# First batch token-major, its value loads moved to the Pool queue ahead of the first weights, second weights in two halves, dummy matmuls at the start

## Chip, cores, metric

One core of a Trainium2 chip. The time is the device time of one execution in microseconds (us), lower is better. Every run of a kernel is correct against the reference unless said otherwise. A ratio is the mean time of one kernel's runs over that of the other's of the same rounds, so it is not quite the ratio of the medians quoted beside it.

## The reference

Forgetting attention, then a gated feed-forward block on its output:

```python
# q, k, v: (8 batches, 8 heads, 576 tokens, 64), f: (8, 8, 576)
scores = scale * q @ k.T
cum    = cumsum(log(clip(f, 1e-4, 1.0)))
scores = where(causal, -1e9, scores + cum_i - cum_j)
attn   = exp(scores - max); attn = attn / (sum + 1e-9)
x      = (attn @ v) reshaped to (4608 tokens, 512)
gate   = sigmoid(x @ w_gate)          # 512 x 1536
out    = (gate * (x @ w_val)) @ w_out # 1536 x 512
```

## The kernel before

It is scheduled by hand: the order of the program text is the order on each engine's queue. Scores are computed transposed (keys on partitions), ACT takes the exp, Pool (GpSimd) masks the diagonal blocks, PE multiplies with values that DVE or Pool scaled by the decay. The attention of the first batch runs alone (the opening); then each later batch is woven into the feed-forward chunks of 512 tokens, step by step. Loads with a cast from float32 to bf16 are issued by Pool, in line with its masks.

```python
def load_w1(c0, c1):                 # two issues on Pool
    cs = slice(c0, c1)
    for src, part in ((moe_w_gate, LO), (moe_w_val, HI)):
        nc.gpsimd.dma_start(w1[part, :, cs], src.rearrange("(s p) c -> p s c", p=64)[:, :, cs])

def load_w2(gi):                     # one issue on Pool: output weights "wo"
    nc.gpsimd.dma_start(wo[:, 4 * gi:4 * gi + 4, :], ...)

def S_unit(p, u, slot, tag=None):    # one unit of scores of head pair p
    ...                              # matmuls into ps
    nc.scalar.activation(e[...], ps[...], ACTF.Exp, scale=scale)
    nc.gpsimd.affine_select(out=m, in_=m, ...)      # the mask, on Pool

# the opening
nc.sync.dma_start(f_nat, ...)
load_v(0, 0, 4, range(NJT), nc.sync)        # values of heads 0-3 on SP
load_qk(0, 0, ((0, 2), (2, 4)))             # Pool
make_identity(nc, ident_bf)
load_qk(0, 1, ((0, 4),))
make_identity(nc, ident_f)
load_v(0, 4, 8, range(NJT), nc.gpsimd)      # values of heads 4-7 on Pool
load_w1(0, 512)
... (four pairs: units U, V, W; sums and values with tokens on columns) ...
load_w1(1024, 1536)

# the weave of the first chunk; put(step, what)
put(12, rest_values)                        # PE needs the masked eD, eA, eB of the rest units
for x, w in enumerate((5, 9, 12)):
    put(w, lambda x=x: load_w2(x))          # on Pool, between masks
```

A 64-token rest of each pair (unit Z, tiles eD, eA, eB, eC) is computed in the weave.

The softmax here doesn't subtract the row's maximum and nothing guards it: scores larger than these inputs give would overflow.

## Time and profile before

| | before |
|---|---|
| time | 374.13 us median of 3 (373.37 to 374.95) |
| span of the profiled execution | 373.4 us, granted clock 0.998 |
| PE busy | 359.3 us (96%) |
| opening ends (transposes of the second batch begin on PE) | 28.6 us |
| first sigmoid on ACT | 28.50 us |

The prediction below shows the stages, the chain of waits and the timeline of the opening. Two more views of this kernel are needed later. First, the page's line of the chain that ended last, by engine, which says that almost nothing but PE sets the end:

```profile
PE 94%; ACT 2%; DMA 1%; issue 1%; DVE 1%; POOL 0%; ACTq 0%; POOLq 0%
```

Second, the timeline of Pool at the first output weights (columns: start us, length us, engine, line, operation, out<-in, shapes, count, and in brackets the idle time before it and what ended it):

```profile
33.97 0.76 POOL L155 DMA_DIRECT2D wo<-in_moe_w_out_dram  x1 [2.09 <-DMA w<-in_moe_w_val_dram]
...
37.92 0.29 POOL L248 TENSOR_SCALAR_AFFINE_SELECT eB<-eB 64x128 bf16<-64x128 bf16 x1 [0.39 <-ACT eB L246]
```

Pool stands still 2.09 us before it can issue the load of wo, until a load of w issued earlier (at 24.91) has landed. The masks stand behind it in the same queue. Here it costs nothing: the last eB mask is waiting for ACT, not for Pool, and PE begins `rest_values` at 37.90 in one burst.

### The profile page before, as it was taken

How to read it: one execution, taken by the hardware profiler on the slowest of the kernel's cores; microseconds unless marked ns; L12 is line 12 of the kernel's file. 1: busy time of each engine (PE TensorE's matmuls, PEld its weight loads, DVE VectorE, ACT ScalarE, POOL GpSimd, SP SyncE). 2: the span in 40 equal slices, each digit the busy share in tenths (PEclk: the TensorE clock that was granted, in tenths of full speed). 3: DMA queues.
4: the chain of work that ended last, by engine and by line, in shares of the span. 5: the costliest groups of instructions: out<-in, count | busy, mean ns of one | idle time of the engine just before them, and what ended most of it. 6: DMA issues, size and time to landing. Idle time of an engine off the chain costs nothing.

```text
span 373.4 us, 12210 instructions
## 1 busy us (share of the span) xinstructions
PE 359.3 (96%) x5259; PEld 192.0 (51%) x5264; DVE 176.5 (47%) x382; ACT 195.7 (52%) x294; POOL 168.3 (45%) x265
## 2 busy tenths in 40 slices
PE   2889999999999999999999999999999999999996
PEld 1547545455555545454665566545456544444442
DVE  5775482557375555274708370737064703312320
ACT  5868754574736472848374727471747313323321
POOL 8896745064826663559665946460415000000000
PEclk9999999999999999999999999999999999999999
DMA  8999999599988976789984996596313131011002
GB/s 157 233 209 256 194 182 217 173 213 154 158 164 196 157 84 63 168 182 134 142 185 105 185 177 138 148 159 83 99 59 76 32 102 58 3 56 58 0 24 90
DMA packets 101350, 49.24 MB, mean 132 GB/s; under 512 B 72001, under 2 KB 94401, under 8 KB 101297
## 3 DMA queue, kind: packets, MB, share of 16 engines
q0 software_dynamic: 48704, 20.65, 44.0%
q1 hardware_dynamic: 52448, 27.68, 30.8%
q8 instruction: 41, 0.67, 0.8%
q10 hardware_dynamic: 144, 0.13, 0.1%
q14 instruction: 13, 0.10, 0.1%
HBM read 37.90 MB, written 9.44 MB: 127 GB/s over the span
## 4 chain that ended last, share of the span: by engine, by line
PE 94%; ACT 2%; DMA 1%; issue 1%; DVE 1%; POOL 0%; ACTq 0%; POOLq 0%
PE ps L455 51%; PE ps L495 17%; PE ps L352 8%; PE ps L504 8%; PE ps L241 6%; PE ps L195 2%; PE ps L300 1%; DMA qk_in<-in_k_dram 1%; ACT eC L246 1%; ACT eB L246 0%; ACT eA L246 0%; ACT kT L200 0%; PE ps L417 0%; DVE kT L200 0%; POOL qk_in L97 0%
## 5 line engine op out<-in xcount | busy, mean ns | idle before, releaser
L455 PE MATMUL ps<-xR,w 64*128 64x512 bf16 x1728 | 205.1, 376 | 0.2
L465 DVE SCALAR_TENSOR_TENSOR gv<-sg,ps 128x512 bf16<-128x512 bf16 x108 | 74.0, 686 | 152.2 <-ACT sg L464 149.0
L455 PEld LDWEIGHTS <-w 64*128 64x128 bf16 x1728 | 86.2, 94 | 84.0 <-issue 2.5
L464 ACT ACTIVATE sg<-ps 128x512 bf16<-128x512 f32 x108 | 64.5, 598 | 85.1 <-PE ps L455 83.9
L248 POOL TENSOR_SCALAR_AFFINE_SELECT eC<-eC 128x256 bf16<-128x256 bf16 x32 | 12.9, 404 | 94.4 <-ACT eC L246 94.4
L241 PE MATMUL ps<-qT,kT 64*128 64x320 bf16 (+6 forms) x416 | 47.0, 275 | 2.0 <-ACT kT L200 1.1
L246 ACT ACTIVATE eC<-ps 128x896 bf16<-128x896 f32 (+1 forms) x32 | 28.1, 878 | 20.7 <-PE ps L241 20.4
L257 POOL TENSOR_TENSOR vg<-vb,g_bf 128x640 bf16<-128x640 f32 x30 | 37.8, 1261 | 0.0
L482 ACT ACTIVATE ob<-ps 128x512 f32<-128x512 f32 x35 | 19.6, 596 | 32.2 <-PE ps L504 20.1
L495 PE MATMUL ps<-wox,gvx 64*128 64x512 bf16 x288 | 35.7, 376 | 0.0
L241 PEld LDWEIGHTS <-kT 64*128 64x128 bf16 x416 | 22.9, 96 | 24.0 <-issue 4.9
L246 ACT ACTIVATE eA<-ps 128x896 bf16<-128x896 f32 (+2 forms) x33 | 30.5, 926 | 9.0 <-PE ps L241 8.5
L495 PE MATMUL ps<-wo,gv 64*128 64x512 bf16 x288 | 34.4, 376 | 0.0
L246 ACT ACTIVATE eB<-ps 128x768 bf16<-128x768 f32 (+2 forms) x33 | 27.4, 832 | 10.0 <-PE ps L241 9.2
L504 PE MATMUL ps<-wo,gv 128*128 128x512 bf16 x140 | 32.1, 380 | 0.3 <-issue 0.2
L271 DVE TENSOR_TENSOR xR<-ps,R 128x64 bf16<-128x64 f32 (+2 forms) x68 | 26.2, 429 | 2.1
L108 POOL DMA_DIRECT2D vb<-in_v_dram x30 | 25.2, 849 | 0.2 <-issue 0.2
L263 DVE STREAM_TRANSPOSE R<-r 128x576 f32<-128x576 f32 (+1 forms) x32 | 24.6, 770 | 1.1
L495 PEld LDWEIGHTS <-gvx 64*128 64x128 bf16 x288 | 15.7, 94 | 13.0 <-issue 0.4
L495 PEld LDWEIGHTS <-gv 64*128 64x128 bf16 x288 | 15.3, 94 | 13.7 <-issue 0.5
L246 ACT ACTIVATE eD<-ps 128x640 bf16<-128x640 f32 x30 | 21.1, 702 | 2.0 <-PE ps L241 2.0
L504 PEld LDWEIGHTS <-gv 128*128 128x128 bf16 x144 | 13.4, 98 | 16.7 <-issue 1.4
(82 smaller groups left out, 325.9 us busy)
## 6 DMA issues: line engine op xcount, KB each, us to landing
out_dram<-ob SPq DMA_DIRECT2D x35, 256.0 KB, 2.2
vb<-in_v_dram POOLq DMA_DIRECT2D x20, 256.0 KB, 5.4
xR<-xR SPq DMA_DIRECT2D x20, 144.0 KB, 4.1
gvx<-gv SPq DMA_DIRECT2D x12, 192.0 KB, 4.8
vb<-in_v_dram SPq DMA_DIRECT2D x8, 256.0 KB, 7.3
k_rows<-in_k_dram POOLq DMA_DIRECT2D x16, 128.0 KB, 6.0
q_rows<-in_q_dram POOLq DMA_DIRECT2D x16, 128.0 KB, 5.6
qk_in<-in_q_dram POOLq DMA_DIRECT2D x7, 288.0 KB, 6.7
```

The costliest lines, as they stand in the source:

```text
L108: eng.dma_start(vbs[b % 2][0:n, t, h0:h1, :], rows)
L241: nc.tensor.matmul(ps[:, sc + h, c:c + i1 - i0], k_at(p, jt)[hp, :], qT[hp, i0:i1], start=True, stop=True)
L246: nc.scalar.activation(e[:, :, 0:w], ps[:, sc:sc + 2, 0:w], ACTF.Exp, scale=scale)
L257: (eng or nc.gpsimd).tensor_tensor(out=vg[:, :, :, 0:D], in0=vbs[b % 2][:, :, 2 * a:2 * a + 2, :], in1=g_bf[:, :, 2 * p:2 * p + 2].unsquee ...
L263: nc.vector.transpose(R.rearrange("p (n c) -> p n c", c=32), r.unsqueeze(2).to_broadcast([128, r.shape[1], 32]))
L271: nc.vector.tensor_tensor(out=xR[:, a, r0:r0 + n], in0=psf[:, o + i:o + i + n], in1=R[:, i:i + n], op=ALU.mult)
L352: nc.tensor.matmul(psf[32 * qd:32 * qd + 32, o + a:o + z], lhsT_of(jt, qd), e_of(u, qd)[:, c:c + z - a], start=(y == 0), stop=(y == len(to ...
L455: nc.tensor.matmul(ps[:, bk, :], w1[half, head, ft * NP:(ft + 1) * NP], xR[half, sl, t0:t0 + TCH], start=(first and x == 0), stop=(last an ...
L464: nc.scalar.activation(sg, ps[:, fb, :], ACTF.Tanh, scale=0.5)
L465: nc.vector.scalar_tensor_tensor(out=gv[:, ft, :], in0=sg, scalar=1.0, in1=ps[:, fb + 1, :], op0=ALU.add, op1=ALU.mult)
L495: nc.tensor.matmul(ps[:, bk, :], lhsT, rhs, start=(x == 0 and ft == 0), stop=(x == 1 and ft == NFT - 1))
L504: nc.tensor.matmul(ps[:, 4 + tt, :], gv[:, ft, tt * NP:(tt + 1) * NP], wo[:, ft, :], start=(ft == 0), stop=(ft == NFT - 1))
```

## The change

Its intent: the sums come out as an extra column of the values, so for each pair DVE's two stream transposes and the separate sum matmuls go, and with them the three half swaps; dummy matmuls at the start are to raise PE's clock before the first scores; the first keys share the DMA engines with less.

```diff
-    load_v(0, 0, 4, range(NJT), nc.sync)
     load_qk(0, 0, ((0, 2), (2, 4)))
-    make_identity(nc, ident_bf)
-    load_qk(0, 1, ((0, 4),))
-    make_identity(nc, ident_f)
-    load_v(0, 4, 8, range(NJT), nc.gpsimd)
-    load_w1(0, 512)
+    ... memsets on DVE, identities on Pool ...
+    busy(10, 3)                               # ten dummy matmuls of 512 columns
+    load_v(0, 0, H, (NJT - 1,), nc.sync)      # only the last 64 rows on SP
+    load_v_pair(0, 0)
+    load_qk(0, 1, ((0, 4),))
+    load_v_pair(0, 1)
 ...
     T_step(0, 4, ACTC, DVEC)
+    nc.scalar.activation(gT, cum, ACTF.Exp, ...)
+    load_v(0, 4, 8, (0, 1), nc.gpsimd)
+    S_unit(0, "U", 0)
 ...
     for p in range(HPAIR):
-        S_unit(p, "U", p % 2)
-        S_unit(p, "V", 1 - p % 2)
-        if p + 1 < HPAIR:
-            T_step(p + 1, 4, DVEC, ACTC)
-        if p:
-            burst = out_one(p - 1, 6, 7)      # sums, transposes, values, scaling
+        main_unit(p, 1)
+        if p == 0:
+            load_v(0, 4, 8, (2, 3), nc.gpsimd)
+        elif p == 2:
+            load_w1(512, 768)
+        if p > 1:
+            back_main(p - 2)                  # 8 transposes back, DVE copy, SP crossing
 ...
+        main_unit(p, 2)
+        if p == 0:
+            load_w1(0, 512)
+        elif p == 1:
+            load_qk(1, 0, ((0, 4),))
+        if p:
+            vals_main(p - 1, 6, EARLY + LATE) # 40 matmuls of 65 columns
+            norm_main(p - 1, 6)               # reciprocal and scaling on DVE
 ...
+    load_w1(768, 1024)
     load_w1(1024, 1536)
-    swap(1, 0) ... swap(2, 1) ... swap(3, 2)
+    ... 8 transposes and copies for each of pairs 2 and 3, in place of the swaps ...
```

The cut leaves out two more dummies (`busy(2, 4)`, in the round of the second pair). From step 4 of the first chunk on the program text is unchanged.

## The prediction

> **What bounds the kernel now.** I read the page first, then the busy time by stage, then the chain of waits and the timeline of the first 30 us, because the diff touches nothing after the fourth step of the first feed-forward chunk.
>
> The page's busy row and the table by stage (columns: window, length, then busy us and count of each engine, granted clock, DMA share, GB/s):
>
> ```profile
> PE 359.3 (96%) x5259; PEld 192.0 (51%) x5264; DVE 176.5 (47%) x382; ACT 195.7 (52%) x294; POOL 168.3 (45%) x265
> ```
>
> ```profile
> 8.00:10.00 2.00, 1.79 (x46) 1.09 (x45) 0.72 (x3) 1.13 (x3) 2.00 (x4) 1.00 1.23 217
> 10.00:12.00 2.00, 0.95 (x6) 0.28 (x7) 1.93 (x5) 1.90 (x3) 1.34 (x3) 1.00 1.20 257
> ...
> 20.00:22.00 2.00, 1.50 (x24) 0.93 (x20) 1.75 (x4) 2.00 (x3) 2.00 (x5) 1.00 1.22 214
> 22.00:24.00 2.00, 2.00 (x27) 0.99 (x23) 1.33 (x3) 0.78 (x2) 2.00 (x4) 1.00 1.22 220
> ...
> 28.60:40.00 11.40, 11.29 (x232) 8.03 (x232) 5.88 (x10) 9.43 (x15) 6.44 (x14) 1.00 1.17 248
> 60.00:200.00 140.00, 139.17 (x2363) 75.86 (x2364) 73.13 (x168) 78.23 (x117) 78.41 (x116) 1.00 1.00 159
> ```
>
> PE is busy 359.3 of 373.4 us. From 28.6 us on it is the bound (11.29 of 11.40, 139.17 of 140.00). Of the 14.1 us in which it is idle, the rows up to 28.6 us hold some 8.8. Only there can this change earn anything.
>
> The chain of waits of that opening (start, length, what):
>
> ```profile
> 2.07 4.61 DMA qk_in<-in_k_dram
> 6.72 0.71 PE ps L195 x28
> 7.46 0.77 DVE kT L200
> ...
> 9.85 1.02 ACT eB L246
> ...
> 13.29 1.27 PE ps L300 x10
> ...
> 20.17 0.69 PE ps L300 x10
> 20.87 0.73 DVE Z L319
> 21.62 0.74 PE ps L300 x10
> 22.35 0.32 PE ps L332
> ...
> 28.68 0.43 PE ps L195 x36
> ```
>
> The reader sees three phases: to 6.7 us the first keys are awaited; to about 22 us softmax work alternates between ACT and PE; from 22.35 to 28.6 PE is dense with the last sums, values, half swaps and the first weight slots. The same ten matmuls of L300 take 1.27 us at 13.29 and 0.69 at 20.17: PE runs at about half speed until some 16.7 us although the granted clock reads 1.00.
>
> The timeline gives the other engines of this phase:
>
> ```profile
> 8.93 1.02 ACT L246 ACTIVATE eA<-ps 128x1024 bf16<-128x1024 f32 x1 [0.87 <-PE ps L241]
> 21.59 0.60 ACT L246 ACTIVATE eC<-ps 128x512 bf16<-128x512 f32 x1
> 22.47 0.40 POOL L248 TENSOR_SCALAR_AFFINE_SELECT eC<-eC 128x256 bf16<-128x256 bf16 x1
> 37.90 0.51 PE L417 MATMUL ps<-vg,eD 128*64 128x65 bf16 x20
> ```
>
> ACT starts its first exp at 8.93 and ends the twelfth at 22.19: 13.26 us for 4 x (1.02 + 1.02 + 0.62) + 3 x 0.65 = 12.6 us of work. So ACT, and Pool with its masks behind it (last one ends 22.87), pace the middle phase; PE paces the end of it.
>
> [...] The trace shows a DMA share of about 1.2 from 4 us to 28 us at some 210 GB/s, so moving a load between SP and Pool buys no bandwidth, only order.
>
> **The change part by part.**
> Token-major values: for each head pair the 10 sum matmuls and 10 value matmuls (0.69 + 0.74 us warm, 1.27 + 1.21 cold) become 40 matmuls of 65 columns with the sum as last column. The nearest row, L417 with 40 such, spans 0.81 us. Added are 8 transposes for each pair, 8 more for pairs 2 and 3, 48 in all; at the 0.43 us of 36 small transposes (12 ns each) to twice that for 128 columns, 0.1 to 0.25 us for each eight. Removed are three swaps of 0.32. On PE: before 4 x 1.43 + 0.96 = 6.7 us, after 4 x 0.81 + 6 x 0.25 = 4.7, and 0.44 for two idle-filling matmuls: 1.5 us less.
> DVE: stream transpose 0.71, reciprocal 0.25, transpose 0.71, scaling 0.69 = 2.4 us for each pair become reciprocal about 0.2, scaling about 0.7, copy about 0.5 = 1.4. The four scalings of values (0.9 to 1.1 with their column copy) are all on DVE now, two more than before; Pool loses two of 1.5 us.
> Ten dummy matmuls of 512 columns at the start: L300's cold burst streams 512 + 2 x 256 + 2 x 128 = 1280 columns in 1.27 us, two heads beside each other, so 512 take at most 0.5 us (the first page gives 0.43), from about 1.3 to 5.6 or 6.4 us, while nothing else can run. They end about when the first keys land, and should leave PE warm some 10 us earlier.
> Order of loads: on SP only the forget gates and the last 64 rows of values remain (272 KB, before 720), so the first keys share less. Estimate 5.6 to 6.5 us for their landing against 6.68. The second half of q and k comes behind 256 KB of values on Pool, while 576 KB left SP: estimate 10.5 to 11.9 us at 0.22 MB/us, against 11.29 for the queries before. It is wanted at about 12. The first weights are issued at about 13 instead of 9.9 and should land near 20, and are wanted at about 22.5. The halved second weights cost two more Pool issues (2 x 0.69) and change no byte.
> ACT: the exp of the decay (0.77) now stands behind the first query copy (0.64), not before it. The table load still ends at 6.2, so ACT: copy to 7.0, decay to 7.8, first exp at 7.8 to 8.5. Plus 12.6 us without a stall: last exp ends 20.4 to 21.1, against 22.19.
> Pool: from 1.32 us: 4 q/k issues 2.6, identities 0.5, v pair 1.46, q/k 1.26, v pair 1.46, two v 1.46, masks of the first two units 1.07, two v 1.46, mask 0.4, two weights 1.4, three masks 1.47, q/k 1.25, two masks 1.07, two weights 1.4, four masks 1.9 = 20.2 us, so the last mask ends at 21.5, against 22.87. Pool is by this count the latest of the engines, although it lost two scalings: the four v issues that stood on SP are now its own.
> The end of the opening on PE, in its new order, from the mask of the fourth pair's second unit (about 21.1): early values 0.25, sixteen transposes 0.45, the 28 late value matmuls 0.57 (not before 21.5), two slots of weights 0.43, eight transposes 0.25, four slots 0.86, eight transposes 0.25, six slots 1.3, the rest unit 0.15, four slots 0.86 = 5.4, and about 0.5 for the wait for DVE (norm 0.6, copies 0.3) that stands between: 27.0. Before, the same point (transposes of the second batch) was 28.61.
>
> Sum: 1.6 us earlier. After it the instruction order on PE, ACT and DVE is the same and PE is dense, so the gain is carried to the end: 374.13 - 1.6 = 372.5, and I take a little more for keys at the early end of their range: 372.3.
>
> **The rivals.**
> First, the crossed halves of pair 1, now by SP DMA instead of a PE swap. They leave after DVE's copy at about 19.8. The same DMA before took 5.6 us to land. Landing 25.4 to 26, wanted at 25.2: it could hold PE for up to 1 us. The time would be 373 to 373.5. For it: a saturated DMA. Against it: six slots stand ahead of it.
> Second, the first weights. They start 3 us later behind more values; 9.9 us to landing for the second half of them before, from 13.8, is 23.7, past the 22.5 that PE wants. That would cost about 1 us too. Against it: the queue before them has drained by then.
> Third, the clock. PE has less work and waits more, so it may be cold when the dense end begins: five us of work would take up to 2.5 more, and the gain is gone (374 to 375). Against it: the masks come every 0.5 us[...].
> Fourth, better than thought: ACT, not Pool, paces it, if Pool's issues overlap or are shorter; last mask 20.8, PE's end 25.3 and the time 370.8.
> Fifth, the weights that come later (columns from 1024) land some 32 us and are wanted at about 40, so no new wait is due there; a miss would show as PE waiting on w.
>
> **Range and chances.** The ideal opening, with ACT never waiting, is worth 3.3 us; the three bad rivals take 1 to 2.5 each, partly overlapping. Runs of the kernel before spread over 1.6 us. So 370.7 to 374.0 for eight in ten. Two per cent is 7.5 us, more than a quarter of the opening: faster by that 0.02, slower 0.01.
>
> **What would show it.** The point where the second batch's transposes start on PE: right if 26 to 28 us. First exp on ACT at 7.8 to 8.5; last at 20.4 to 21.2; last mask of the four pairs near 21.5. Matmuls of 512 columns at warm speed by 7 us. PE busy over the span lower by some 1.5 us less the 4.5 of dummies, that is, higher. It is wrong if PE waits for xR or w by DMA between 22 and 28 us, if the rows after 28 us show new idle time on PE, or if Pool's last mask is later than 22.5.

The sum came to 27.0 against 28.61 us, 1.6 us earlier, so 374.13 - 1.6 = 372.5, and 372.3 with the keys early. That the dummies would bring PE's full speed forward, and that waiting might lose it again, was not shown by the trace before. "No bandwidth, only order" rests on that trace: 222 GB/s from 4 to 8 us, with the queue of Pool's loads at 71.5% of the 16 engines and that of SP's at 50.7%, and 209 GB/s from 22 to 28 us, with 116.2% and 6.1%. The 0.43 us for 512 columns can be read there too: L300's two matmuls of 512 columns start at 13.22 us and the next ones at 13.65.

## The result and the profile after

| | before | after |
|---|---|---|
| time, median of 4 runs each | 374.44 us | 379.12 us (378.72 to 379.93) |
| ratio | | 1.0131, 95% interval 1.0102 to 1.0161 |
| profiled span, granted clock | 373.4 us, 0.998 | 377.2 us, 0.991 |
| transposes of the second batch begin on PE | 28.6 us | 28.5 us |

The kernel became 1.3% slower; the predicted time was 372.3 and the range ended at 374.0. It stayed within 2%, which had the greatest chance, but it went the other way and past the range.

The page of the changed kernel, its busy row, its row of the granted clock (40 equal slices, in tenths) and the chain by engine:

```profile
PE 362.1 (96%) x5396; PEld 190.9 (51%) x5401; DVE 175.4 (46%) x386; ACT 195.1 (52%) x295; POOL 170.0 (45%) x264
...
PEclk9699999999999999999999999999999999999999
...
PE 86%; POOL 7%; DMA 3%; issue 1%; ACT 1%; DVE 0%; POOLq 0%; ACTq 0%
```

POOL went from 0% to 7% and DMA from 1% to 3% of the chain. 10% of 377 us is about as long as the time to the end of `rest_values`: the chain through the opening and up to 41 us is now one of Pool and a DMA. The clock row falls to 6 in its second slice, 9.4 to 18.9 us.

The table by stage, for answering the prediction's rows (columns as there):

```profile
8.00:10.00 2.00, 1.32 (x49) 1.00 (x49) 1.18 (x3) 2.00 (x3) 2.00 (x4) 0.85 1.00 150
...
14.00:16.00 2.00, 2.00 (x48) 1.49 (x48) 1.12 (x3) 1.03 (x3) 2.00 (x4) 0.50 0.71 102
...
28.60:40.00 11.40, 9.88 (x214) 5.39 (x214) 5.38 (x8) 8.51 (x14) 6.12 (x12) 1.00 1.22 242
```

Three things are to be seen. Pool (the fifth pair) is busy 1.97 to 2.00 us of each 2 us from 8 to 24 us. At 14 to 16 us the granted clock is half and the DMA engines carry 102 GB/s, where before they carried 208: little is queued for them, because Pool comes late to issue it (the first weights at 13.71 us, before at 9.88). And from 28.6 to 40 us PE is busy 9.88 of 11.40 us, before 11.29.

The column of the granted clock must be read with care. In these two traces its record begins with the first stretch of full clock, and up to there it reads 1.00. In the kernel before that is at 17.1 us, and PE is at half speed up to there, as the prediction saw (1.27 against 0.69 us for the same matmuls). In the changed kernel the record begins at 6.0 us, so its half clock from 9.4 to 16.2 us is on record. These two stretches are 3.413 us and twice that long; a "window" below is such a stretch of 3.41 us. The mean clocks of the two kernels (0.998 and 0.991) therefore don't say that the changed kernel ran slower on PE in the opening.

The chain of waits (start, length, what), cut to the pieces that matter:

```profile
20.82 1.15 POOL eB L258
...
24.28 12.95 DMA w<-in_moe_w_val_dram
...
40.54 0.56 POOL eB L258 x2
...
41.15 0.22 PE ps L470 x2
```

Up to 24.28 every piece but some short ones of issue is Pool's. Then a load of w takes 12.95 us to land; only then can Pool issue wo (at 37.52), and only then come the masks of eC, eD, eA, a second wo (at 39.79) and the masks of eB that PE needs. The timeline shows the same from the engines' side:

```profile
7.96 1.02 ACT L256 ACTIVATE eA<-ps 128x1024 bf16<-128x1024 f32 x1
...
10.11 1.27 DVE L267 TENSOR_TENSOR vg<-vb,g_bf 128x640 bf16<-128x640 f32 x1
...
10.58 1.29 POOL L258 TENSOR_SCALAR_AFFINE_SELECT eB<-eB 128x512 bf16<-128x512 bf16 x1
...
20.64 0.60 ACT L256 ACTIVATE eC<-ps 128x512 bf16<-128x512 f32 x1
...
21.92 0.41 POOL L258 TENSOR_SCALAR_AFFINE_SELECT eC<-eC 128x256 bf16<-128x256 bf16 x1
...
37.52 0.77 POOL L163 DMA_DIRECT2D wo<-in_moe_w_out_dram  x1 [1.76 <-DMA w<-in_moe_w_val_dram]
...
41.15 0.22 PE L470 MATMUL ps<-vg,eB 128*64 128x65 bf16 x2 [0.95 <-POOL eB L258]
...
51.67 0.21 PE L405 MATMUL ps<-eB,vg 128*32 128x64 bf16 x3 [1.67 <-issue]
```

The first and last exp and the last mask came within 0.9 us of where they were predicted. Why does the load of wo, which needs nothing of w, wait for a load of w? The traces tell it. In all fourteen of them together, each of the 64 waits of a Pool issue for a DMA that the timelines show up to 64 us ends with the landing of the eighth issue before it. Eight places before the first wo stands the last load of w, in both kernels. So in these traces an issue waits until the issue eight places before it has landed, and at most eight loads from Pool are in flight. Whether the chip or the way the program is built sets this number, no run shows.

PE waits for masks (0.77 for eD, 0.48 for eA and 0.95 for eB), and it stands still 1.67 us in the middle of a burst of short matmuls with nothing to wait for that the profile shows, "issue".

To add this up I set the ACT instructions of the two traces beside each other, from the first sigmoid on, where their order is the same, and took the difference of their starts:

| up to | lag of after | added there |
|---|---|---|
| first sigmoid (28.5) | -0.15 us | -0.15: the opening |
| last exp before the masks (37) | -0.14 | 0 |
| next exp (39.1 against 41.7) | +2.64 | +2.8: PE waits for masks |
| 44.6 against 47.2 | +2.52 | -0.1 |
| next sigmoid (49.7 against 53.8) | +4.06 | +1.5: the gap marked "issue" |
| end | +3.60 | -0.5: single steps of 0.2 to 0.8 both ways |

So there are three questions: why the opening gained nothing, why the masks came late, and what the gap marked "issue" is.

For the gap, the view of the DMA queues in a 2-us stretch (queue, kind: packets, MB, share of 16 engines). After, from 48 to 50 us:

```profile
q0 software_dynamic: 369, 0.37, 118.2%
q8 instruction: 1, 0.02, 3.0%
```

Before, from 46 to 48 us:

```profile
q0 software_dynamic: 140, 0.15, 81.6%
q8 instruction: 1, 0.02, 2.8%
```

A queue named "instruction" brings one packet of 16 KB. There are 41 of them for 10,523 PE instructions (matmuls and weight loads) in the kernel before and 42 for 10,797 in the changed one, one for each 257. In both kernels one comes in this stretch, while Pool issues six loads of queries and keys. In the kernel before, with the engines at 81.6%, it begins at 46.13 us and PE loses 0.13 us near it (48.48); in the changed kernel, with the engines at 118.2%, it begins at 49.39 and PE stands still from 50.01 to 51.67. Counted from the start of the program, the gap comes after 1,469 PE instructions in the kernel before and after 1,724 in the changed one. In these two and in the eight other runs that show a gap, the number leaves 188 to 190 over a multiple of 256. I call such a place a block boundary, what lies between two of them an instruction block, and a gap there a block gap. That PE waits there for its next instructions is my reading; e_phase below tests whether the gap goes with the count.

### The profile page after: what moved, and what is told of

It is laid out like the page before. It is cut to its first block, busy times and chain, and to the rows that moved or that the text cites. A ratio compares the mean times of both kernels' runs of the same rounds, so it can differ in the third digit from the quotient of the medians.

```text
span 377.2 us, 12482 instructions
## 1 busy us (share of the span) xinstructions
PE 362.1 (96%) x5396; PEld 190.9 (51%) x5401; DVE 175.4 (46%) x386; ACT 195.1 (52%) x295; POOL 170.0 (45%) x264
## 4 chain that ended last, share of the span: by engine, by line
PE 86%; POOL 7%; DMA 3%; issue 1%; ACT 1%; DVE 0%; POOLq 0%; ACTq 0%
PE ps L508 47%; PE ps L548 16%; PE ps L557 8%; PE ps L405 8%; PE ps L249 5%; DMA w<-in_moe_w_val_dram 3%; POOL w L160 1%; POOL qk_in L99 1%; PE ps L203 1%; POOL eB L258 1%; POOL vb L115 1%; POOL vb L110 1%; POOL eA L258 1%; ACT eC L256 0%; POOL eC L258 0%
## 5 line engine op out<-in xcount | busy, mean ns | idle before, releaser
L508 PEld LDWEIGHTS <-w 64*128 64x128 bf16 x1728 | 84.4, 94 | 84.6 <-issue 1.3
L267 POOL TENSOR_TENSOR vg<-vb,g_bf 128x640 bf16<-128x640 f32 x28 | 35.3, 1262 | 0.0
L249 PEld LDWEIGHTS <-kT 64*128 64x128 bf16 x416 | 21.9, 95 | 24.2 <-issue 4.0
L256 ACT ACTIVATE eA<-ps 128x896 bf16<-128x896 f32 (+2 forms) x32 | 29.4, 923 | 6.9 <-PE ps L249 6.4
L256 ACT ACTIVATE eB<-ps 128x768 bf16<-128x768 f32 (+2 forms) x32 | 26.3, 827 | 10.0 <-PE ps L249 9.2
L281 DVE TENSOR_TENSOR xR<-ps,R 128x64 bf16<-128x64 f32 (+2 forms) x64 | 23.5, 413 | 1.7
L256 ACT ACTIVATE eD<-ps 128x640 bf16<-128x640 f32 x30 | 21.1, 702 | 5.3 <-PE ps L249 5.3
L273 DVE STREAM_TRANSPOSE R<-r 128x576 f32<-128x576 f32 x28 | 21.8, 779 | 1.0
```

Of the source, the lines that this page charges most:

```text
L249: nc.tensor.matmul(ps[:, sc + h, c:c + i1 - i0], k_at(p, jt)[hp, :], qT[hp, i0:i1], start=True, stop=True)
L256: nc.scalar.activation(e[:, :, 0:w], ps[:, sc:sc + 2, 0:w], ACTF.Exp, scale=scale)
L267: (eng or nc.gpsimd).tensor_tensor(out=vg[:, :, :, 0:D], in0=vbs[b % 2][:, :, 2 * a:2 * a + 2, :], in1=g_bf[:, :, 2 * p:2 * p + 2].unsquee ...
L273: nc.vector.transpose(R.rearrange("p (n c) -> p n c", c=32), r.unsqueeze(2).to_broadcast([128, r.shape[1], 32]))
L281: nc.vector.tensor_tensor(out=xR[:, a, r0:r0 + n], in0=psf[:, o + i:o + i + n], in1=R[:, i:i + n], op=ALU.mult)
L508: nc.tensor.matmul(ps[:, bk, :], w1[half, head, ft * NP:(ft + 1) * NP], xR[half, sl, t0:t0 + TCH], start=(first and x == 0), stop=(last an ...
```

## The experiments

Theory at the start: Pool's queue is the cause. All the value issues stand in it, so weights start later (13.71 us against 9.88), their DMA lands later, and the masks stand behind an issue that waits for that landing. The rivals: bandwidth (the order of the loads, whoever issues them), the clock that the dummies upset, the halves of the second weights, and the instruction blocks as a cost of their own. All runs were timed in five rounds beside the kernel before (374.02 to 374.77 us median in these rounds). "Lag" is the alignment of ACT described above, in the profiled execution. It is one execution each: the changed kernel, e_wo_late and e_wo_early have the same program up to step 4, and their first sigmoids lag by -0.15, 0.47 and 0.88 us; e_no_dummy and e_nodummy_wo too, with 0.06 and -0.72. Differences of less than about 1 us in the opening are therefore not read as effects.

| run | median us | ratio to before, 95% | lag: first sigmoid / after masks / after burst |
|---|---|---|---|
| changed kernel | 379.12 | 1.0131 [1.0102, 1.0161] | -0.15 / 2.64 / 4.06 |
| e_wo_late | 378.50 | 1.0116 [1.0071, 1.0160] | 0.47 / 0.46 / 1.64 |
| e_v_on_sp | 378.94 | 1.0134 [1.0113, 1.0154] | 1.97 / 2.75 / gap 2.04 |
| e_phase | 378.51 | 1.0125 [1.0087, 1.0162] | 0.87 / 2.90 / gap 1.64 later |
| e_one_piece | 379.20 | 1.0135 [1.0117, 1.0153] | 1.15 / 2.75 / gap 1.60 |
| e_no_dummy | 378.99 | 1.0110 [1.0084, 1.0135] | 0.06 / 3.15 (4.19 next) / no gap |
| e_warm | 378.67 | 1.0106 [1.0085, 1.0126] | 1.58 / 3.41 / gap 1.00 |
| e_warm_wo | 376.62 | 1.0051 [1.0026, 1.0076] | 1.06 / 1.05 / gap 2.46 |
| b_v_on_pool | 377.49 | 1.0079 [1.0058, 1.0101] | 1.75 / 2.97 / no gap |
| e_nodummy_wo | 374.53 | 1.0013 [0.9991, 1.0036] | -0.72 / -0.70 / -0.67 |
| e_w_first | 379.42 | 1.0149 [1.0124, 1.0174] | 3.65 / 3.64 / 4.16 |
| b_dummy | 375.49 | 1.0033 [1.0011, 1.0055] | 0.26 / 0.26 / 1.66 |
| e_wo_early | 377.11 | 1.0071 [1.0042, 1.0100] | 0.88 / 0.87 / 2.82 |

### e_wo_late: output weights issued later

```diff
-    for x, w in enumerate((5, 9, 12)):
+    for x, w in enumerate((13, 14, 16)):
```

> The changed kernel with its three loads of the output weights (wo) issued at steps 13, 14 and 16 of the first chunk instead of 5, 9 and 12; nothing else. Mask theory: in the changed kernel PE waits 2.6 us between 37.8 and 41.3 us because four masks of Pool stand in line behind the wo load, whose issue waits (37.5 us) for the landing of the last weights. With the loads behind the masks the wait of PE goes: 2.3 us earlier from step 14 on, ratio to before about 1.007 (376.8 us). Contention theory (the masks themselves are slow, or PE waits for something else there): PE still waits about 2.5 us and the ratio stays 1.013. If the 1.7 us gap of PE at 50 us, seen as issue, is set by transfers in flight, it may move or change here; if by the count of PE instructions it stays.

The ratio was to be 1.007 by the one theory and 1.013 by the other; its interval, 1.0071 to 1.0160, holds both, so the trace must decide. The lag stays at 0.46 us across step 12: with no issue of wo in front of the masks, the wait is gone, and so it was that issue that held them. But the issues now stand in front of other masks, and the burst of 120 short matmuls waits:

```profile
47.58 0.29 PE L405 MATMUL ps<-eD,g_bf 128*32 128x256 bf16 x3 [1.22 <-POOL eD L258]
```

The timed executions fell into two groups: spans of 374.1 to 375.1 us with a mean clock of 0.986 or 0.991, and 378.5 to 379.5 with 0.980 or 0.981. The profiled execution is one of the first group. Taking one wait away is thus not enough, and the clock has a part that the profile of one execution cannot size.

### e_v_on_sp: the first batch's values all on SP

```diff
-    load_v(0, 0, H, (NJT - 1,), nc.sync)
-    load_v_pair(0, 0)
+    load_v(0, 0, H, range(NJT), nc.sync)
     load_qk(0, 1, ((0, 4),))
-    load_v_pair(0, 1)
 ...  (both later load_v(0, 4, 8, ...) on Pool dropped)
```

> The changed kernel with all values of the first batch loaded by SP at the start (five transfers of 8 heads), so Pool issues eight loads fewer. Serial Pool theory: Pool's 8 issues of about 0.75 us are what delays the first weights (issued 13.7 us instead of 9.9), leaves the DMA engines half idle between 12 and 16 us and makes the last weights land 3.3 us late; here the first weights are issued before 9.5 us, the last land before 34.5, PE waits less than 1 us for masks at 38 us, and the opening ends 1 us earlier too: ratio 1.000 to 1.006. Rival (bandwidth): the bytes are the same and the first keys and the second half of q and k now share with 1.2 MB of values, so they land later by 1 us or more and the opening gains nothing: ratio 1.008 to 1.015.

Pool is relieved of eight issues, and the opening becomes 1.97 us longer, not shorter: the values now share the DMA engines with the first keys, of which the second load lands at 7.29 us in place of 6.12. The wait at the masks shrinks to 0.60 us for eB, as PE comes later. In the simple form (free Pool, win the opening) my theory failed; the bandwidth rival was right for the opening. The run did not test an earlier start of the weights: they were issued at 12.86 us, not before 9.5 as I expected, because masks stand before them in the program.

### e_phase: 128 more PE instructions at the start

```diff
     busy(10, 3)
+    for _ in range(64):
+        nc.tensor.matmul(ps[:, 3, 0:16], spare[:, 0:NP], spare[:, 0:16], start=True, stop=True)
```

> The changed kernel with 64 matmuls of 16 columns more (128 PE instructions with their weight loads) behind the ten at the start, where PE has little to do; cost there at most 2 us, partly hidden by the wait for the first keys. Fetch theory: the 1.7 us gap of PE at 50 us, in the middle of a burst of 240 short instructions, is PE waiting for its own instructions (16 KB blocks come at 39.4 and 49.4 us); shifting the stream by half a block moves the fetch to another place and the gap at that burst shrinks below 0.4 us, another gap may appear elsewhere. Rival: the gap is set by DMA traffic or a semaphore; it stays at the same burst with 1.2 us or more. Ratio by the first 1.009 to 1.014, by the second 1.013 to 1.018.

Each matmul is two PE instructions, weights and product (5,401 and 5,396 of them in the changed kernel). The gap of 1.67 us left the burst of L405 and stood elsewhere:

```profile
55.37 0.82 PE L508 MATMUL ps<-xR,w 64*128 64x512 bf16 x6 [1.64 <-issue]
```

It begins at 53.73, where the count again leaves 188 to 190 over a multiple of 256; the mask wait stayed. So the gap goes with the count of PE instructions, not with the burst.

### e_one_piece: the second weights in one piece

```diff
-            load_w1(512, 768)
+            load_w1(512, 1024)
 ...
-    load_w1(768, 1024)
```

> The changed kernel with the second weights (columns 512 to 1024) loaded in one piece at the third pair, as one pair of transfers; undoes one part of the change and takes away two of Pool's issues (1.4 us). Mask theory with late DMA as its root: the transfers start about 4 us earlier with more bytes, so the engines are fed, the last weights land 1 to 2 us earlier than 37.2, and PE's wait for masks falls by as much; ratio 1.007 to 1.011. Rival: the halves don't matter, since what is late was late by 16 us already: ratio 1.012 to 1.014, the last weights land at 37 us as before.

The halves are not the cause: 1.0135, wo issued at 37.65 as before in the changed kernel (37.52), though the packets of the stretch from 24 to 34 us fell from 3118 to 2137.

### e_no_dummy: no dummy matmuls

```diff
-    busy(10, 3)
 ...
-            if p == 1:
-                busy(2, 4)
```

> The changed kernel without its twelve dummy matmuls. In the changed kernel the clock record shows full speed for one window (6.0 to 9.4 us), then half speed until 16.2 us (19.7 in other runs), so the dummies bought 3.4 us of full speed in a phase in which PE waits anyway. Clock theory[...]: without dummies PE is cold until 16 to 20 us, and the opening (first sigmoid of the feed-forward, 28.35 us) ends at 28 to 30.5; ratio 1.010 to 1.017, little different from the changed kernel. Rival (the dummies are what costs: they hold PE while the first keys could be turned): the opening ends over 0.5 us earlier, below 27.8, and the ratio falls under 1.010.

The opening is as long as before (+0.06), without dummies. PE is at half speed up to 17.0 us, as in the kernel before, only that no record of it begins earlier (36 small transposes take 0.70 us at 9.61 us and 0.48 at 17.03). The block gap is gone: with 24 PE instructions fewer the boundary no longer falls into the burst. But the mask wait is 3.1 us, and half clock follows it. The stages of this run around it (last three columns: granted clock, DMA share, GB/s):

```profile
40.00:42.00 2.00, 0.88 (x16) 0.59 (x18) 0.18 (x1) 0.00 (x0) 1.41 (x4) 0.73 1.20 202
42.00:44.00 2.00, 2.00 (x14) 0.69 (x12) 0.42 (x1) 0.70 (x1) 1.01 (x2) 0.50 1.25 208
```

The clock is half from 40.9 to 44.3 us, and the lag grows by another 1.04. So removing the dummies alone gave nothing clear of noise, 1.0110.

### e_warm: more dummies in PE's waits

```diff
     T_step(0, 4, ACTC, DVEC)
+    busy(3, 6)
 ...
-            if p == 1:
-                busy(2, 4)
+            if p:
+                busy((5, 3)[p - 1], 4)
 ...
         if p < 3:
+            if p == 0:
+                busy(4, 6)
             main_unit(p + 1, 0)
```

> The changed kernel with ten dummy matmuls more, in places where PE waits in the trace: three after the first turn of q and k, four before the second pair's first scores, three more before the third pair's turn, three before the fourth's. Clock theory: PE's windows between 6 and 16 us stay busy, the half-speed stretch shrinks or goes, the opening ends 1 to 2 us earlier (26.3 to 27.5 us at the first sigmoid). The mask wait at 38 us is set by the landing of the last weights on DMA and doesn't move in time, so PE gives the gain back there: it waits for masks 3.5 to 4.5 us instead of 2.3, and the total stays: ratio 1.011 to 1.014. Rival (PE's speed in the opening is not what holds it; ACT and Pool are): the opening ends at 28 to 29 us as before with full clock throughout.

The clock was full from 5.8 to 22.9 us (in the changed kernel from 6.0 to 9.4) and then half to 26.3, just in the dense end. The opening was to become 1 to 2 us shorter and became 1.58 longer, so this expectation failed. The last mask came no earlier (it starts at 22.51, in the changed kernel at 21.92). That the middle phase is held by Pool and not by PE's speed fits this; the ten more dummies also take time on PE, and the run does not part the two.

### e_warm_wo: the same dummies, output weights at steps 11, 12, 16

```diff
-    for x, w in enumerate((5, 9, 12)):
+    for x, w in enumerate((11, 12, 16)):
     (and the edit of e_warm)
```

> The same ten dummies, and the three loads of the output weights at steps 11, 12 and 16, each behind the masks of its step. If both causes are as I think (clock lost in the opening, masks behind a load that waits), the opening is 1 to 2 us shorter than in the kernel before and PE waits less than 1 us for masks until 60 us, and where PE no longer runs into the burst at 50 us with the last q/k loads in flight its fetch gap is below 0.5 us: ratio 0.994 to 0.999. If the masks are now held by the landing of the first output weights or by the values of the second batch instead, or if the fetch gap stays: 1.000 to 1.006.

No mask wait at all, and the ratio falls from 1.0106 to 1.0051, as in the second case of the expectation; the opening is 1.06 us longer, not shorter, and the block gap is 2.46 us, the longest seen.

### b_v_on_pool: one part alone, on the kernel before

```diff
-    load_v(0, 0, 4, range(NJT), nc.sync)
     load_qk(0, 0, ((0, 2), (2, 4)))
     make_identity(nc, ident_bf)
+    load_v(0, 0, 4, range(NJT), nc.gpsimd)
     load_qk(0, 1, ((0, 4),))
```

> The kernel before with one part of the change alone: the values of the first four heads of the first batch go from SP to Pool's queue, behind the first q and k and ahead of the second half. Queue theory (what stands on Pool ahead of the weights costs time later on): Pool's first masks come 3 us later, the first weights are issued about 3.5 us later (13.4 instead of 9.9 us), the last weights land 1 to 3 us later than 33.9 and PE waits for masks at 38 us by up to 2 us: ratio 1.003 to 1.010. Rival (Pool has slack in this kernel; the change's loss comes with the token-major form and its clock): ratio 0.999 to 1.002.

Moving the values to Pool, without any token-major code, brings the same kind of wait into the kernel before:

```profile
41.48 0.22 PE L417 MATMUL ps<-vg,eB 128*64 128x65 bf16 x2 [0.94 <-POOL eB L248]
```

The first weights are issued at 13.60 and wo at 37.87, as in the changed kernel. The 1.75 us of its opening is partly of its own making: PE waits 3.6 us for the small identity, which now stands behind the loads on Pool.

### e_nodummy_wo: no dummies and output weights at steps 11, 12, 16

```diff
-    busy(10, 3)
 ...
-            if p == 1:
-                busy(2, 4)
 ...
-    for x, w in enumerate((5, 9, 12)):
+    for x, w in enumerate((11, 12, 16)):
```

> The changed kernel without its dummy matmuls and with the three output-weight loads issued at steps 11, 12 and 16 (changed kernel: 5, 9, 12). Theory (the loss after the opening is the mask wait behind the waiting Pool issue plus a late instruction block, and the opening itself is worth next to nothing): no PE wait for eD, eA or eB of more than 0.3 us between 37 and 42 us, first sigmoid within 0.4 us of the kernel before, the clock full from about 17 us on; ratio to the kernel before 0.998 to 1.003 if the instruction block comes in time, 1.003 to 1.006 with one gap of 1 to 2.5 us at 48 to 53 us. Rival (the token-major form is dearer by itself all along, whatever stands on Pool): ratio stays at 1.008 or more.

This takes the whole loss away: 374.53 us, ratio 1.0013, interval 0.9991 to 1.0036. Pool's timeline shows the masks ahead of the load:

```profile
37.22 0.29 POOL L258 TENSOR_SCALAR_AFFINE_SELECT eB<-eB 64x128 bf16<-64x128 bf16 x1 [0.31 <-ACT eB L256]
37.47 0.76 POOL L163 DMA_DIRECT2D wo<-in_moe_w_out_dram  x1
```

The eB mask now waits for ACT only, as in the kernel before. No gap stands at the burst. The first sigmoid comes 0.72 us earlier than before (more than the 0.4 I allowed), and 0.67 of it is still there after the burst; in e_no_dummy, with the same opening, nothing of this shows. The rival, that the token-major form is dearer by itself all along, is ruled out. That it is cheaper is not shown either: the interval holds 1.

### e_w_first: first weights issued ahead of the last values

```diff
-    load_v(0, 4, 8, (0, 1), nc.gpsimd)
+    load_w1(0, 512)
     S_unit(0, "U", 0)
 ...
-            load_v(0, 4, 8, (2, 3), nc.gpsimd)
+            load_v(0, 4, 8, (0, 1), nc.gpsimd)
 ...
-            load_w1(0, 512)
+            load_v(0, 4, 8, (2, 3), nc.gpsimd)
```

> The changed kernel with the first weights' two issues moved ahead of the last four value loads on Pool (issued at about 8.5 us, as before or earlier). Theory (what made the output-weight issue wait until 37.2 us is that the weights start 3.8 us later and behind starved DMA engines): the last first weights and the following loads land 2 to 4 us earlier, the wait of PE for the masks at step 12 shrinks from 3.5 us to under 1.5, ratio 1.004 to 1.010. Rival (the same bytes are in flight whichever comes first, so the last load before the output weights lands at the same time): the mask wait stays at 2.5 us or more and the ratio at 1.012 or more. In either case a wait of DVE for the late values may appear at 17 to 21 us.

No faster, 1.0149, against the theory's 1.004 to 1.010. The last values took 7.50 us to land (13.73 to 21.23), DVE waited for them, the clock was half from 22.2 to 29.0 us, and the opening grew by 3.65. The mask wait is gone, but because PE comes 3.65 us later: wo was issued at 36.54, only 1.0 us earlier than 37.52, not the 2 to 4 us that I expected. As a test of when the late landing arises it is inconclusive.

### b_dummy: only the ten dummies, on the kernel before

```diff
     load_qk(0, 0, ((0, 2), (2, 4)))
+    nc.vector.memset(spare, 1.0)
+    for _ in range(10):
+        nc.tensor.matmul(ps[:, 3, :], spare[:, 0:NP], spare, start=True, stop=True)
     make_identity(nc, ident_bf)
```

> The kernel before with only the ten dummy matmuls added at its start. Theory (the dummies buy one window of full clock at about 6 to 9.5 us and the clock is then lost again, so they are worth nothing): the opening within 0.5 us of the kernel before, the clock row low at 10 to 16 us, ratio 0.998 to 1.003. Rival of the change's intent (a clock kept from 6 us on shortens the first transposes and first scores): opening 1 us or more shorter and ratio 0.995 to 0.998.

1.0033, a hair above the 1.003 of the theory. The opening is 0.26 us longer, not shorter. The mean clock of five of its six executions is 0.986 to 0.991, the level of the changed kernel, against 0.998 to 1.000 of the kernel before. That fits an early window of full clock and a stretch of half clock after it, which is then on record; these five were not profiled. The profiled execution is the sixth: its record begins at 17.7 us, so the ten dummies bought it no early window. The 20 PE instructions move the block boundary into the burst here as well:

```profile
49.27 0.21 PE L352 MATMUL ps<-eB,vg 128*32 128x64 bf16 x3 [1.53 <-issue]
```

### e_wo_early: output weights at steps 11, 12, 16, dummies kept

```diff
-    for x, w in enumerate((5, 9, 12)):
+    for x, w in enumerate((11, 12, 16)):
```

> The changed kernel with the output-weight loads issued at steps 11, 12 and 16 and nothing else changed (the dummy matmuls stay). It splits the run without dummies and with these steps (ratio 1.0013) into its two parts. Theory (the moved loads take the mask wait away, 2.6 us; the dummies cost by the clock windows they upset in the opening and by 20 PE instructions that bring the instruction block into the dense run): no mask wait over 0.3 us between 37 and 42 us, first sigmoid 0 to 1.3 us later than in the kernel before, one gap of 1 to 2.5 us at 46 to 54 us, ratio 1.003 to 1.008. Rival (the dummies are without effect and the loads are all): ratio 0.999 to 1.003. Second rival (the loads alone do nothing, as in the run with steps 13, 14, 16): 1.010 or more.

1.0071: no mask wait, the first sigmoid 0.88 us late with half clock from about 9 to 19 us, and a block gap of 2.03 us. Its executions again fall in two groups (spans of 373.7 to 374.7 at clocks 0.989 to 0.991, 376.1 to 376.9 at 0.986). All as the theory had it. Moving the loads is worth 0.6% alone, leaving out the dummies 0.2% alone (their intervals overlap), both 1.2%. That the two need each other is not shown: by the four intervals 1.2 is not clearly more than 0.6 + 0.2. With the loads moved, leaving out the dummies is worth 0.6%, clear of noise.

## Why the prediction was wrong

**The shorter first keys, the first and the last exp: right.** First exp 7.96 (predicted 7.8 to 8.5), the twelfth ends at 21.24 (20.4 to 21.2). PE did not wait for xR or w from 22 to 28.5 us, so the first two rivals stayed away; the second part of the first weights landed at 23.2 and was used from 23.69. (The 9.9 us that the second rival took for it is the median of such loads; the one meant took 8.6.)

**Pool as the latest engine: right, its sum too short by 0.8.** The last mask ends at 22.33, predicted 21.5. The term that was mis-sized is the mask of two blocks: 1.29 and 1.15 us for two of the four eB masks, where I counted 0.6 to 0.7 for each. Both began while DVE was scaling values (vg<-vb,g_bf), which the change moved wholly to DVE. In the fourteen traces 16 eB masks of the opening began so with 0.39 to 0.82 us of the scaling left; each ended 0.49 to 0.50 us after it and took 0.89 to 1.31 us. The other 29 took 0.63 to 0.74.

**The end of the opening on PE, "27.0": wrong by 1.5, in two terms.** By my sum the first feed-forward matmuls were due at 21.1 + 0.25 + 0.45 + 0.57 + 0.5 = 22.87; they began at 23.69. The sixteen transposes took some 0.73 us from start to the next matmul (22.39 to 23.12), not 0.45, and stood behind the late mask. From there to the end I had 4.1 us, and it took 4.81 (23.69 to 28.50): the slots of 4, 8 and 12 matmuls need 0.53, 0.97 and 1.51 us between them and their successors and eight transposes 0.35, where I took 0.43, 0.86, 1.3 and 0.25. Without dummies the same point is at 27.93 in e_nodummy_wo and at 28.71 in e_no_dummy, whose opening is the same program: of the 1.6 us, between nothing and 0.7 was there.

**The dummies "should leave PE warm some 10 us earlier": wrong.** They bought one window: full clock from 6.0 to 9.4 us, half from 9.4 to 16.2, where the kernel before is at half speed up to 17.1. In other executions the half clock lasts longer (to 19.5 in e_one_piece). What loses the full clock is not shown: it ended after windows in which PE was busy 2.28 of 3.41 us (changed kernel, 6.0 to 9.4), about 2.1 (e_warm), 1.7 (e_w_first) and 1.6 (e_no_dummy), and stayed after one of 2.16 us (changed kernel, 36.7 to 40.1). No single busy share tells these apart. The third rival (a cold PE at the dense end) did not come in the changed kernel, where the clock is full from 16.2 on; it came in e_warm, with half clock from 22.9 to 26.3. Without dummies the opening is no longer (e_no_dummy 0.06, changed kernel -0.15).

**"The gain is carried to the end", and the fifth rival "no new wait is due there": this is the step that failed most.** I asked when PE would want the later weights and found it safe. PE never waited for w. I didn't ask what on Pool waits for their landing. The profile of before showed it: 2.09 us of Pool's idle time, ended by w, right in front of wo, with the masks of `rest_values` behind it. The first weights started 3.8 us later. The last ones were issued no later than before (24.28 against 24.91), but behind more unfinished loads: their landing, which frees Pool, moved from about 33.7 to 37.2, and PE lost 2.8 us. That moving wo behind the masks removes exactly this wait is shown by three runs (e_wo_late, e_warm_wo, e_wo_early) and by the sum of e_nodummy_wo; that values on Pool bring it, by b_v_on_pool.

Why the landing moved by 3.5 us can be followed in the bytes: summing rate by length over the stages from 1 to 34 us gives 7.16 MB for the kernel before and 6.28 MB for the changed one. Of the 0.88 MB missing, 0.50 are lost from 8 to 16 us, where Pool had queued too little; at 205 GB/s that is 2.4 us of the 3.5, as an estimate. Another 0.32 are missing from 24 to 34 us, but these are no second loss. The rates of that stretch in forty slices, before and after:

```profile
GB/s 197 209 217 205 201 213 201 213 201 213 188 188 197 197 205 213 197 213 217 205 201 197 217 201 205 209 209 201 213 201 258 365 365 418 287 287 369 328 311 344
...
GB/s 188 211 247 216 197 222 232 224 203 193 199 256 182 178 186 197 195 197 191 191 197 201 199 199 199 207 205 213 209 201 215 201 209 205 205 258 197 188 197 205
```

Up to 31 us both move some 205 GB/s. Then the kernel before is through with the weights and moves the next values, in packets of 4 KB in place of 1 KB, at some 340 GB/s; the changed kernel comes to them at 35 us (320 GB/s from 35 to 38, before 217). The halves change nothing here, as e_one_piece found. That the starved stretch is the cause of the late landing is argued from the traces; e_w_first, meant to test it, did not settle it.

**The instruction block: not in the prediction at all.** 1.5 us. At one boundary PE lost 0.64 to 2.46 us in nine kernels and 0.13 us in the kernel before. That it goes with the count of PE instructions is shown (moved by e_phase, gone in e_no_dummy and e_nodummy_wo, brought into the kernel before by b_dummy). What sets its size is open. The packet itself took 0.89 to 1.04 us in all ten traces that have the gap, and PE went on 1.3 to 1.7 us after its end, with more loads in flight or fewer. What differs is how long before PE stood still the packet began: 2.35 us in the kernel before (gap 0.13), 0.62 in the changed one (1.67), 0 in e_warm_wo (2.46). Whether loads in flight delay its start, no run isolates.

**What the issues cost.** That a load moved between SP and Pool changes only the order agrees with e_v_on_sp, where values on SP made the first keys land 1.2 us later (7.29 against 6.12). I let the issues pass as a mere term of a sum. Here each issue up to 25 us took 0.62 to 0.81 us of an engine that also makes the masks, and in the changed kernel Pool was busy without a break of 0.1 us from 4 to 24 us.

What stays open besides: the two groups of executions in e_wo_late and e_wo_early, and how much of the timed 1.3% is clock, gap or wait in executions that were not profiled.

## What to carry to other kernels

When loads are moved to an in-order queue, look at everything behind them, above all at an issue that already waits for an earlier load to land. It need not be a load of the same data: here it was the issue eight places before. A wait that costs nothing today has a slack, and the slack is the number to compare the delay with (here about 0.7 us: the landing moved by 3.5 and PE lost 2.8). Two small repairs that were worth 0.6% and an unclear 0.2% alone, other places for three issues and no dummy matmuls, removed the whole loss together, so test them together before giving up on either. Before two mean clocks are compared, see where their records begin. A gap marked "issue" in a burst of short matmuls may go with the count of PE instructions: add or drop a few early and see whether it moves (here 128 more moved it from 50.01 to 53.73 us).
